# Transposing q and k of six batches on TensorE instead of by DMA, in an attention and GeGLU kernel

## The chip, the core and the metric

The kernel runs on one core of a Trainium2 chip. The core has TensorE (matmul; the trace shows its weight loads apart from its matmuls), VectorE, ScalarE, GpSimd and SyncE, which all run at once, each with an instruction queue of its own, and 16 DMA engines that serve the transfers that SyncE, ScalarE and GpSimd issue. The metric is the device time of one execution in microseconds (us).

## The reference

Two steps are computed. First comes attention with a sliding window and a linear distance bias, for 8 batches of 8 heads, 576 positions and a head size of 64; then a GeGLU block on the 4608 tokens.

```python
scores = (1/sqrt(64)) * q @ k.T
rel = pos[:, None] - pos[None, :]
scores = where((rel >= 0) & (rel < 128), scores - slope[h] * abs(rel), -1e9)
attn = softmax(scores)
x = (attn @ v)            # then laid out as [4608 tokens, 512]
out = (gelu(x @ w_gate) * (x @ w_val)) @ w_out    # 512 -> 1536 -> 512
```

All inputs and the output are float32; the kernel computes in bfloat16 with sums in float32.

## The kernel before

The tokens are cut into nine groups g of 512 (`NG`). For each group, a gate stage runs twelve steps f (`gate_val`, L615): eight matmuls of 512 columns each make 128 rows of the gate and the value, ScalarE applies gelu and VectorE multiplies, into `hid[g]`. After the gate stage comes a list of steps (`todo` for groups 0 and 1, `steps` for the others, L910 to L924). Numbers in the list are units of three output matmuls (`out_part`, L662); the named steps are the attention of later batches. In the list of group g from 2 on these are the weighted values of batch g + 1 (`pv`) and the scores of batch g + 2 (`s2`), so attention is ahead of the GeGLU block.

q and k of a batch are loaded by GpSimd in natural layout into `qs[b % 2]` and `ks[b % 2]`: five tiles of 128 positions, the fifth with 64, by 512 channels. The scores need them with channels on the partitions, as `qT[b % 2]` and `kT[b % 2]`: four column blocks c of 128 channels (two heads each) by 576 positions.

Batches 0 and 1 are transposed on TensorE, against the identity, at the start (`transpose`, L166, `first`, `rest`). For batches 2 to 7 `transposes_dma` (L173) issues six DMA transposes for a batch on SyncE's queue: five for q, one for each tile of 128 positions (L182), and one for k (L175), which lays the k blocks out by tile, so that `keys` (L195) picks them in another way. All five tiles are moved whole, so GpSimd first clears the unused 64 rows of the fifth (L904, L967). Batch 2 is transposed in the list of group 0, batch 3 at the start of group 1, and batch g + 2 at the start of group g, for g from 2 to 5.

The two buffers for each operand order the loads. GpSimd issues the loads of a later batch behind a small copy to `mark`, which waits for something: for the transposed q of batch 2 (L976) before the loads of batch 3, for the transposed k of batch 3 (L938) before those of batch 4, and for the product of step f = 9 (L960) before the later ones. In the same gate stages stand the sums of the softmax (`sums4`), their gathering and spreading by DMA on ScalarE's queue, and the loads at f = 9.

All matmul results go to eight banks of PSUM (`bank`, L68), one tile for each call; a bank is given out again when its last reader is done. The instructions run on each engine in the order written (a manual schedule); the framework adds the waits. SyncE's queue also carries the stores of the output (L659) and the small relays (L208) by which one half of a bank is handed from one pair of matmuls to another.

Of the kernel before, what the change touches and what calls it, by code (L numbers as in the profile page):

```python
# [8 lines left out]
BF16 = mybir.dt.bfloat16  # L9
# [23 lines left out]
def kernel(  # L33
# [10 lines left out]
    nc = tc.nc  # L44
    B, H, S, D = q.shape
# [22 lines left out]
    def bank():  # L68
        return psum.tile([128, 512], FP32, name="ps")


    def keep_busy(ps, n, w=64, rhs=None):
        for _ in range(n):
# [7 lines left out]
    ident = consts.tile([128, 128], BF16, name="ident")  # L81
# [11 lines left out]
    mark = consts.tile([1, 2], BF16, name="mark")  # L93
    last = consts.tile([128, DM], FP32, name="last")

    qs, ks = ([consts.tile([128, 5, DM], BF16, name=f"{nm}s{i}") for i in range(2)]
              for nm in "qk")
    qT, kT = ([consts.tile([128, 4, 640], BF16, name=f"{nm}T{i}") for i in range(2)]
              for nm in "qk")
    vb = [consts.tile([128, 5, DM], BF16, name=f"vb{i}") for i in range(2)]  # L100

    def rows(j):
        return 64 if j == 4 else 128
# [4 lines left out]
    def load(t, src, b, js=range(5), last=0):  # L108
        for j in js:
            n = rows(j)  # L110
            at = last if j == 4 else 0
            nc.gpsimd.dma_start(  # L112
                out=t[at:at + n, j, :].rearrange("p (h d) -> p h d", h=H),
                in_=src[b][:, 128 * j:128 * j + n, :].rearrange("h p d -> p h d"))

    def load_qk(b):
        load(qs[b % 2], q, b)
        load(ks[b % 2], k, b)

    def load_v(b, js=range(5)):  # L120
        load(vb[b % 2], v, b, js, 64)
# [44 lines left out]
    def transpose(b, what, c, copy):  # L166
        ps = bank().bitcast(BF16)
        for n, lo in ((0, 0), (1, 384)):
            transpose_runs(b, n, what, c, ps[:, lo:576])
        for n, lo in ((0, 0), (1, 384)):  # L170
            untangle(copy, b, n, what, c, c + 1, ps[:, lo:576])

    def transposes_dma(b):  # L173
        def of_k():
            nc.sync.dma_start_transpose(  # L175
                out=kT[b % 2].rearrange("p c (j t) -> p (c j) t", t=128),
                in_=ks[b % 2].rearrange("p j x -> p (j x)"))

        if b > 3:
            of_k()  # L180
        for j in range(5):
            nc.sync.dma_start_transpose(  # L182
                out=qT[b % 2][:, :, 128 * j:128 * j + 128], in_=qs[b % 2][:, j, :])
        if b <= 3:
            of_k()


    Ps = [consts.tile([128, H, 896], BF16, name=f"P{i}") for i in range(2)]
# [4 lines left out]


    def keys(b, c, m):  # L195
        if b < 2:
            return kT[b][:, c, 64 * m:64 * m + 64]
        at = 512 * (m // 2) + 128 * c + 64 * (m % 2)
        return kT[b % 2].rearrange("p c x -> p (c x)")[:, at:at + 64]

# [410 lines left out]
    hid = {}  # L613

    def gate_val(g, f, lo=0, hi=512, later=None):  # L615
        if g not in hid:
            hid[g] = h_pool.tile([128, NF, 512], BF16, name="hT")
        t0 = 512 * g % RING
        n = hi - lo

        if n > 256 or lo >= 384:
            pg, pv = bank()[:, 0:n], bank()[:, 0:n]
            order = [(w, ps, c, c == 0) for w, ps in ((wg, pg), (wv, pv)) for c in range(4)]
        else:
            ps = bank()
            pg, pv = ps[:, 0:n], ps[:, n:2 * n]
            order = [(w, ps, c, w is wg and c == 0)
                     for cs in ((0, 1), (2, 3)) for w, ps in ((wg, pg), (wv, pv)) for c in cs]
        cols = ((0, 256), (256, 512)) if (g, f) in HALVED else ((0, n),)
        for w, ps, c, begins in order:  # L630
            for a, e in cols:
                nc.tensor.matmul(  # L632
                    out=ps[:, a:e], lhsT=w[:, c, 128 * f:128 * (f + 1)], rhs=xT[:, c, t0 + lo + a:t0 + lo + e],
                    start=begins and a == 0, stop=(c == 3),
                    skip_group_check=n <= 256 and lo < 384 or len(cols) > 1)

        def act():
            gl = g_pool.tile([128, 512], BF16, name="gelu")
            nc.scalar.activation(out=gl[:, 0:n], in_=pg, func=AF.Gelu)  # L639
            nc.vector.tensor_tensor(out=hid[g][:, f, lo:hi], in0=pv, in1=gl[:, 0:n],  # L640
                                    op=ALU.mult)

        if later is None:
            act()
        else:
            later.append(act)
# [10 lines left out]
    def store():  # L657
        for args in stores:
            nc.sync.dma_start(**args)  # L659
        stores.clear()  # L660
# [63 lines left out]
    for h in (0, 2, 4, 6):  # L724
        for w, src in ((0, q), (1, k)):
            (nc.scalar if w and h == 0 else nc.sync).dma_start(  # L726
                out=raw[w][h // 4].rearrange("p (h x) -> p h x", h=4)[:, h % 4:h % 4 + 2, :],
                in_=src[0][h:h + 2, 0:384, :].rearrange("h (p r) d -> p h (r d)", r=3))
# [42 lines left out]
    def masks_of_last_blocks(lo, hi):  # L771
        nc.vector.tensor_copy(out=emask[:, lo:hi, 192:384], in_=emask[:, lo:hi, 0:192])
        nc.vector.tensor_copy(out=emask[:, lo:hi, 384:512], in_=emask[:, lo:hi, 0:128])
        for x, at in ((0, 128), (1, 0)):
            half = slice(64 * x, 64 * x + 64)
            nc.vector.tensor_copy(out=emask[half, lo:hi, 512:576], in_=emask[half, lo:hi, at:at + 64])


    act, dve = nc.scalar.copy, nc.vector.tensor_copy
# [64 lines left out]
    for do in inverse_a:  # L844
        do[1]()
    dve(out=pairs1.rearrange("p x (h d) -> p h x d", d=64),
        in_=vb[1].rearrange("p j x -> p (j x)")[:, 0:1536].rearrange(
            "p (h x d) -> p h x d", h=H, x=3))
# [6 lines left out]
    masks, waiting = [], []  # L855
# [39 lines left out]
    for n in range(4):  # L895
        nc.gpsimd.dma_start(
            out=wo[:, 3 * n:3 * n + 3, :],
            in_=moe_w_out[384 * n:384 * n + 384, :].rearrange("(c p) f -> p c f", p=128))
# [1 line left out]

    nc.gpsimd.memset(T[64:128, :, 0:64], 0.0)
    nc.gpsimd.memset(Ps[1][:, :, 0:64], 0.0)
    for t in (qs[0], ks[0]):
        nc.gpsimd.memset(t[64:128, 4, :], 0.0)  # L904
    load_qk(2)


    acts = (act, act, act, act)
    scales = []
    todo = {  # L910
        0: [("table",), ("s", 1, 0, (0, 1)), ("o", 0, 0, 0), ("o", 0, 1, 0), ("s", 1, 0, (2, 3)), ("o", 0, 0, 1), ("s", 1, 1, (0, 1)), ("o", 0, 1, 1), ("s", 1, 1, (2, 3), masks), ("pv+", 1, 0), 4, ("transposes", 2), ("pv+", 1, 1), 4],
        1: [("table",), ("s", 2, 0, (0, 1)), 3, ("s", 2, 0, (2, 3)), 2, ("s", 2, 1, (0, 1)), 2, ("s", 2, 1, (2, 3), masks), ("pv+", 2, 0, scales), 1, ("scale",), 2, ("pv+", 2, 1), 1, 2, ("s2", 3, 0), ("add", 3, 0), 3, ("s2", 3, 2), ("add", 3, 2, None, (0,))],
    }

    def steps(g):
# [11 lines left out]
    def exp_table():  # L927
        nc.scalar.preload_act_table_set("natural_log_exp_and_others")

    RUN = {"s": scores, "s2": scores2, "add": add, "sum4": sums4, "gather": gather, "spread": spread_dma, "pv": values, "pv+": values_and_sums,  # L930
           "masks": flush, "table": exp_table, "transposes": transposes_dma, "last": out_last, "scale": lambda: scales.pop()(), "o": out_half}

    for g in range(NG):
        if 1 <= g < B - 2:
            transposes_dma(3 if g == 1 else g + 2)
        if g == 1:

            nc.gpsimd.tensor_copy(out=mark, in_=kT[1][0:1, 0, 512:514])  # L938
            load_qk(4)
            load_v(3)  # L940
        for f in range(9 if g == 0 else 0, NF):
            gate_val(g, f)
            if g == 2 and f == 2:
                add(3, 2, act, (1,))
            if g == 0 and f == 10:
                masks_of_last_blocks(0, 8)
            if g == 0 and f == 9:
                for c in range(4):
                    for w in (0, 1):
                        transpose(1, w, c, (act, dve)[w])  # L950
            if 2 <= g < B - 1:
                if f == (4 if g == 2 else 3):
                    sums4(g + 1)
                if f == (6 if g == 2 else 5):
                    gather(g + 1)
                if f == (8 if g == 2 else 7):
                    spread_dma(g + 1)
                if f == 9 and g + 2 < B:

                    nc.gpsimd.tensor_copy(out=mark, in_=hid[g][0:1, f, 0:2])  # L960
                    if g + 3 < B:
                        load_qk(g + 3)
                    load_v(g + 2)
        if g == 0:
            nc.gpsimd.memset(Ps[0][:, :, 0:64], 0.0)
            for t in (qs[1], ks[1]):
                nc.gpsimd.memset(t[64:128, 4, :], 0.0)  # L967
        for item in steps(g):
            if isinstance(item, int):
                out_part(g, item)  # L970
            else:
                RUN[item[0]](*item[1:])
        store()
        if g == 0:

            nc.gpsimd.tensor_copy(out=mark, in_=qT[0][0:1, 0, 512:514])  # L976
            load_qk(3)
            load_v(2)

# [29 lines left out]
```

## Time and profile before

| what | value |
|---|---|
| median of 3 runs | 338.54 us (338.36 to 339.22) |
| the profiled execution | 337.69 us |
| span of its instructions | 335.9 us |
| TensorE busy | 327.7 us (98%), 3273 matmul records |
| VectorE, ScalarE, GpSimd busy | 192.9, 170.3, 108.3 us |
| granted TensorE clock | 1.00 |
| `qT<-qs` DMA transposes on SyncE's queue | 30, median 1258 ns to issue |
| `kT<-ks` DMA transposes on SyncE's queue | 6, median 3820 ns to issue |

The page of a profile counts how long each engine was busy and follows the chain of work that ended last. A line of a group names the source line, the engine, the operation, the tiles (out<-in), the shape and the number of instructions. For TensorE a form such as 128*64 gives the rows and columns of the array that the instruction uses. Matmuls are pipelined: one lasts 379 ns in the records where the next starts after 216 ns. Some records of matmuls are missing from the trace.

### The profile page before, as it was taken

The numbers are of one execution on the slowest core, as the hardware profiler recorded it, in microseconds if no ns is written. First come the engines' busy times: TensorE is split into PE (matmuls) and PEld (weight loads), VectorE is DVE, ScalarE is ACT, GpSimd is POOL, SyncE is SP. The second block draws the span as 40 slices with busy tenths as digits, with TensorE's granted clock in tenths as the row PEclk, the third lists the DMA queues.
The fourth block names the chain that finished last, engine by engine and source line by source line (L and its number), as shares of the span: only waits on it lengthen the run. The fifth ranks groups of instructions, "written<-read, shape, count | busy, mean of one in ns | idle before, by whom it ended". The sixth has DMA issues, their size and how long they took to land.

```text
span 335.9 us, 8087 instructions
## 1 busy us (share of the span) xinstructions
PE 327.7 (98%) x3273; PEld 169.5 (50%) x3316; DVE 192.9 (57%) x356; ACT 170.3 (51%) x318; POOL 108.3 (32%) x144
## 2 busy tenths in 40 slices
PE   8999999999999999999999999999999999999996
PEld 6667556444554454445544554445444544444444
DVE  7888776445779458845693469546964324303320
ACT  8974687438796339332943275335732233223322
POOL 6974784481193293009400860050000000000000
PEclk9999999999999999999999999999999999999999
DMA  8999999999999899969975999394105110020002
GB/s 216 170 197 191 205 164 189 117 181 137 183 161 153 181 184 198 164 161 134 184 163 104 153 187 179 81 166 83 64 3 140 64 65 0 1 96 31 0 31 96
DMA packets 149914, 43.49 MB, mean 129 GB/s; under 512 B 133588, under 2 KB 142836, under 8 KB 149876
## 3 DMA queue, kind: packets, MB, share of 16 engines
q0 software_dynamic: 107456, 18.10, 70.5%
q1 hardware_dynamic: 39104, 18.62, 25.4%
q10 hardware_dynamic: 3316, 6.25, 7.8%
q8 instruction: 26, 0.43, 0.5%
q14 instruction: 12, 0.10, 0.1%
HBM read 43.65 MB, written 9.53 MB: 158 GB/s over the span
## 4 chain that ended last, share of the span: by engine, by line
PE 94%; issue 2%; DMA 1%; DVE 1%; ACT 1%; SPq 0%; DVEq 0%
PE ps L632 56%; PE ps L669 25%; PE ps L501 5%; PE ps L298 2%; PE ps L689 2%; PE ps L216 1%; DMA qs<-in_q_dram 1%; PE ps L437 1%; PE ps L705 1%; PE ps L154 1%; ACT P L229 0%; SPq L726 0%; DVE xT L537 0%; DVE qT L162 0%; ACT rb L583 0%
## 5 line engine op out<-in xcount | busy, mean ns | idle before, releaser
L640 DVE TENSOR_TENSOR hT<-ps,gelu 128x512 bf16<-128x512 f32 (+3 forms) x117 | 73.6, 645 | 92.6 <-PE ps L632 86.0
L639 ACT ACTIVATE gelu<-ps 128x512 bf16<-128x512 f32 (+3 forms) x117 | 65.0, 564 | 101.7 <-PE ps L632 98.3
L632 PE MATMUL ps<-xT,wv 128*128 128x512 bf16 (+4 forms) x468 | 112.2, 361 | 0.4
L632 PE MATMUL ps<-xT,wg 128*128 128x512 bf16 (+4 forms) x456 | 111.2, 361 | 0.7
L669 PE MATMUL ps<-wo,hT 128*128 128x512 bf16 x375 | 87.6, 379 | 2.1 <-issue 1.4
L632 PEld LDWEIGHTS <-wv 128*128 128x128 bf16 x472 | 45.1, 98 | 48.6
L632 PEld LDWEIGHTS <-wg 128*128 128x128 bf16 x472 | 44.4, 98 | 47.6
L669 PEld LDWEIGHTS <-hT 128*128 128x128 bf16 x396 | 37.0, 98 | 43.4 <-issue 0.3
L229 ACT ACTIVATE P<-ps 128x512 bf16<-128x512 f32 (+1 forms) x108 | 51.3, 581 | 2.0 <-PE ps L216 1.5
L674 ACT COPY osb<-ps 128x512 f32<-128x512 f32 x27 | 15.9, 588 | 50.8 <-PE ps L669 50.8
L232 DVE TENSOR_TENSOR P<-P,emask 128x768 bf16<-128x768 bf16 x60 | 31.2, 555 | 18.2 <-ACT P L229 16.4
L112 POOL DMA_DIRECT2D vb<-in_v_dram x40 | 33.9, 886 | 6.5 <-DMA qs<-in_q_dram 2.3
L112 POOL DMA_DIRECT2D qs<-in_q_dram x30 | 25.2, 858 | 2.3 <-issue 1.8
L112 POOL DMA_DIRECT2D ks<-in_k_dram x30 | 25.4, 894 | 0.1
L960 POOL COPY mark<-hT 1x2 bf16<-1x2 bf16 x4 | 0.7, 174 | 75.7 <-DVE hT L640 75.7
L501 PE MATMUL ps<-P,vb 64*64 64x192 bf16 (+2 forms) x752 | 17.4, 220 | 0.4 <-issue 0.2
L565 DVE TENSOR_TENSOR xT<-ps,rb 128x512 bf16<-128x512 f32 (+3 forms) x34 | 14.6, 501 | 4.6 <-PE ps L501 4.6
L501 PEld LDWEIGHTS <-vb 64*64 64x64 bf16 x752 | 14.8, 107 | 3.6 <-issue 2.8
L385 DVE TENSOR_TENSOR T<-P 64x1024 bf16<-64x1024 bf16 x20 | 13.7, 686 | 0.6
L442 DVE RECIPROCAL r<-ps 128x128 f32<-128x128 f32 (+1 forms) x10 | 9.8, 1019 | 0.0
L298 PEld LDWEIGHTS <-kT 64*64 64x64 bf16 x440 | 7.5, 107 | 4.4 <-issue 4.4
L639 ACT ACT_TABLE_LOAD x7 | 9.0, 1283 | 1.3 <-PE ps L632 1.3
(93 smaller groups left out, 186.4 us busy)
## 6 DMA issues: line engine op xcount, KB each, us to landing
out_dram<-osb SPq DMA_DIRECT2D x35, 256.0 KB
rb<-rd ACTq DMA_DIRECT2D x10, 576.0 KB
vb<-in_v_dram POOLq DMA_DIRECT2D x32, 128.0 KB, 6.5
qs<-in_q_dram POOLq DMA_DIRECT2D x24, 128.0 KB, 5.5
ks<-in_k_dram POOLq DMA_DIRECT2D x24, 128.0 KB, 7.0
wo<-in_moe_w_out_dram POOLq DMA_DIRECT2D x4, 384.0 KB, 12.0
wg<-in_moe_w_gate_dram POOLq DMA_DIRECT2D x5, 256.0 KB, 8.5
wv<-in_moe_w_val_dram POOLq DMA_DIRECT2D x5, 256.0 KB, 9.3
```

Of the source, the lines that this page charges most:

```text
L112: nc.gpsimd.dma_start(out=t[at:at + n, j, :].rearrange("p (h d) -> p h d", h=H), in_=src[b][:, 128 * j:128 * j + n, :].rearrange("h p d -> ...
L229: nc.scalar.activation(out=dst, in_=src, func=AF.Exp, scale=0.125)
L232: nc.vector.tensor_tensor(out=dst, in0=dst, in1=m, op=ALU.mult)
L298: mm = nc.tensor.matmul(out=ps[64 * x:64 * x + 64, col:col + w], lhsT=keys(b, c, m)[half, :], rhs=qT[b % 2][half, c, q0:q0 + w], start=Tru ...
L385: nc.vector.tensor_tensor(out=to[half, :, x:x + 7:2], in0=P[half, :, 0:10:3], in1=P[half, :, 1:11:3], op=ALU.add)
L501: mm = nc.tensor.matmul(out=out, lhsT=lhsT, rhs=prob(b)[half, c, i, col:col + q1 - q0], start=all(t[2] != u for t in todo[:n]), stop=True, ...
L565: nc.vector.tensor_tensor(out=xT[:, c, at:at + e - a], in0=src, in1=recip[b][:, c, a:e], op=ALU.mult)
L632: nc.tensor.matmul(out=ps[:, a:e], lhsT=w[:, c, 128 * f:128 * (f + 1)], rhs=xT[:, c, t0 + lo + a:t0 + lo + e], start=begins and a == 0, st ...
L639: nc.scalar.activation(out=gl[:, 0:n], in_=pg, func=AF.Gelu)
L640: nc.vector.tensor_tensor(out=hid[g][:, f, lo:hi], in0=pv, in1=gl[:, 0:n], op=ALU.mult)
L669: nc.tensor.matmul(out=acc[g], lhsT=hid[g][:, f, 128 * t:128 * (t + 1)], rhs=wo[:, f, :], start=(f == 0), stop=(f == NF - 1))
L674: (nc.vector.tensor_copy if g < B - 2 and t in by_dve.get(g, (0,)) else nc.scalar.copy)(out=osb, in_=acc[g])
```

## The change

`transposes_dma` goes. In its place `transposes(b, c)` transposes column block c of q and of k on TensorE: for each of the two operands it takes a bank, issues five transposes against the identity (four of 128 positions, one of 64) and copies the 576 columns to `qT` or `kT`, the q block on ScalarE and the k block on VectorE (for two blocks of batch 3, both on VectorE). The calls stand in pairs inside gate stages: batch 2 after steps 5 and 7 of group 1, batch 3 after step 11 of group 1 and, one block at a time, in the list of group 1, and batch g + 2 after steps 6 and 8 of group g, for g from 2 to 5. `kT` has one layout for all batches, the clearing of the fifth tile's unused rows goes, and so does the mark before the loads of batch 3. The mark before the loads of batch 4 now waits for the product of step 11 of group 1.

```diff
-    def transposes_dma(b):
-        def of_k():
-            nc.sync.dma_start_transpose(
-                out=kT[b % 2].rearrange("p c (j t) -> p (c j) t", t=128),
-                in_=ks[b % 2].rearrange("p j x -> p (j x)"))
-
-        if b > 3:
-            of_k()
-        for j in range(5):
-            nc.sync.dma_start_transpose(
-                out=qT[b % 2][:, :, 128 * j:128 * j + 128], in_=qs[b % 2][:, j, :])
-        if b <= 3:
-            of_k()
+    def transposes(b, c, copies=None):
+        for w, (src, dst, copy) in enumerate(zip((qs, ks), (qT, kT), copies or (act, dve))):
+            ps = bank().bitcast(BF16)
+            for j in range(5):
+                n = rows(j)
+                nc.tensor.transpose(
+                    out=ps[:, 128 * j:128 * j + n], in_=src[b % 2][0:n, j, 128 * c:128 * c + 128],
+                    identity=ident[0:n, 0:n])
+            copy(out=dst[b % 2][:, c, 0:S], in_=ps[:, 0:S])
...
     def keys(b, c, m):
-        if b < 2:
-            return kT[b][:, c, 64 * m:64 * m + 64]
-        at = 512 * (m // 2) + 128 * c + 64 * (m % 2)
-        return kT[b % 2].rearrange("p c x -> p (c x)")[:, at:at + 64]
+        return kT[b % 2][:, c, 64 * m:64 * m + 64]
...
-    for t in (qs[0], ks[0]):
-        nc.gpsimd.memset(t[64:128, 4, :], 0.0)
     load_qk(2)
...
-        0: [..., ("pv+", 1, 0), 4, ("transposes", 2), ("pv+", 1, 1), 4],
-        1: [("table",), ("s", 2, 0, (0, 1)), 3, ("s", 2, 0, (2, 3)), 2, ("s", 2, 1, (0, 1)), 2, ...],
+        0: [..., ("pv+", 1, 0), 4, ("pv+", 1, 1), 4],
+        1: [("table",), ("s", 2, 0, (0, 1)), 3, ("transposes", 3, 2, (dve, dve)), ("s", 2, 0, (2, 3)), 2, ("transposes", 3, 3, (dve, dve)), ("s", 2, 1, (0, 1)), 2, ...],
...
     for g in range(NG):
-        if 1 <= g < B - 2:
-            transposes_dma(3 if g == 1 else g + 2)
-        if g == 1:
-
-            nc.gpsimd.tensor_copy(out=mark, in_=kT[1][0:1, 0, 512:514])
-            load_qk(4)
-            load_v(3)
         for f in range(9 if g == 0 else 0, NF):
             gate_val(g, f)
+            if g == 1 and f in (5, 7):
+                transposes(2, f - 5)
+                transposes(2, f - 4)
+            if g == 1 and f == 11:
+                transposes(3, 0)
+                transposes(3, 1)
+                nc.gpsimd.tensor_copy(out=mark, in_=hid[g][0:1, f, 0:2])
+                load_qk(4)
+                load_v(3)
+            if 2 <= g < B - 2 and f in (6, 8):
+                transposes(g + 2, f - 6)
+                transposes(g + 2, f - 5)
...
             nc.gpsimd.memset(Ps[0][:, :, 0:64], 0.0)
-            for t in (qs[1], ks[1]):
-                nc.gpsimd.memset(t[64:128, 4, :], 0.0)
...
         if g == 0:
-
-            nc.gpsimd.tensor_copy(out=mark, in_=qT[0][0:1, 0, 512:514])
             load_qk(3)
             load_v(2)
```

More of the change, by code (lines that the diff above doesn't have):

```diff
@@ L910 @@
     todo = {
-        0: [("table",), ("s", 1, 0, (0, 1)), ("o", 0, 0, 0), ("o", 0, 1, 0), ("s", 1, 0, (2, 3)), ("o", 0, 0, 1), ("s", 1, 1, (0, 1)), ("o", 0, 1, 1), ("s", 1, 1, (2, 3), masks), ("pv+", 1, 0), 4, ("transposes", 2), ("pv+", 1, 1), 4],
-        1: [("table",), ("s", 2, 0, (0, 1)), 3, ("s", 2, 0, (2, 3)), 2, ("s", 2, 1, (0, 1)), 2, ("s", 2, 1, (2, 3), masks), ("pv+", 2, 0, scales), 1, ("scale",), 2, ("pv+", 2, 1), 1, 2, ("s2", 3, 0), ("add", 3, 0), 3, ("s2", 3, 2), ("add", 3, 2, None, (0,))],
+        0: [("table",), ("s", 1, 0, (0, 1)), ("o", 0, 0, 0), ("o", 0, 1, 0), ("s", 1, 0, (2, 3)), ("o", 0, 0, 1), ("s", 1, 1, (0, 1)), ("o", 0, 1, 1), ("s", 1, 1, (2, 3), masks), ("pv+", 1, 0), 4, ("pv+", 1, 1), 4],
+        1: [("table",), ("s", 2, 0, (0, 1)), 3, ("transposes", 3, 2, (dve, dve)), ("s", 2, 0, (2, 3)), 2, ("transposes", 3, 3, (dve, dve)), ("s", 2, 1, (0, 1)), 2, ("s", 2, 1, (2, 3), masks), ("pv+", 2, 0, scales), 1, ("scale",), 2, ("pv+", 2, 1), 1, 2, ("s2", 3, 0), ("add", 3, 0), 3, ("s2", 3, 2), ("add", 3, 2, None, (0,))],
     }
@@ L930 @@
     RUN = {"s": scores, "s2": scores2, "add": add, "sum4": sums4, "gather": gather, "spread": spread_dma, "pv": values, "pv+": values_and_sums,
-           "masks": flush, "table": exp_table, "transposes": transposes_dma, "last": out_last, "scale": lambda: scales.pop()(), "o": out_half}
+           "masks": flush, "table": exp_table, "transposes": transposes, "last": out_last, "scale": lambda: scales.pop()(), "o": out_half}
     for g in range(NG):
-        if 1 <= g < B - 2:
-            transposes_dma(3 if g == 1 else g + 2)
-        if g == 1:
-            nc.gpsimd.tensor_copy(out=mark, in_=kT[1][0:1, 0, 512:514])
-            load_qk(4)
-            load_v(3)
         for f in range(9 if g == 0 else 0, NF):
             gate_val(g, f)
+            if g == 1 and f in (5, 7):
[10 more added lines that the diff above has]
+                transposes(g + 2, f - 5)
             if g == 2 and f == 2:
```

## The prediction

> **What bounds the kernel now.** I read the page first: who is busy, and who is on the chain that ends last.
>
> ```profile
> span 335.9 us, 8087 instructions
> PE 327.7 (98%) x3273; PEld 169.5 (50%) x3316; DVE 192.9 (57%) x356; ACT 170.3 (51%) x318; POOL 108.3 (32%) x144
> ...
> PEclk9999999999999999999999999999999999999999
> ...
> PE 94%; issue 2%; DMA 1%; DVE 1%; ACT 1%; SPq 0%; DVEq 0%
> ```
>
> TensorE works without a break and is 94% of the chain; no other engine passes 57%. A busy TensorE can still hide waits, so the waits of its two halves come next (matmuls, then weight loads).
>
> ```profile
> PE ps L669 <- issue: 1.4, 9, 0.2
> ...
> PEld L298 <- issue: 4.4, 11, 0.4
> ...
> PEld L501 <- SPq L209: 0.8, 3, 0.3
> ```
>
> No matmul of the stages waits for a DMA or for qT or kT of batches 2 to 7. The "issue" entries are no stalls: at each the start times show 320 ns in place of 95, which is one matmul record (216 ns) missing. After 20 us I find one stall of over 0.25 us, at 84.8 us. So what the change puts on TensorE inside a gate stage is paid in full, and what it takes from the DMA queues shortens nothing on TensorE. I then looked in the timeline of TensorE for what a transpose costs there, and what stands around it.
>
> ```profile
> 34.80 0.81 PE L632 MATMUL ps<-xT,wv 128*128 128x512 bf16 x3
> 35.55 0.25 PE L154 MATMUL ps<-ident,qs 128*64 128x128 bf16 x2
> ...
> 37.36 0.42 PE L154 MATMUL ps<-ident,ks 128*64 128x128 bf16 x10
> 37.72 0.39 PE L632 MATMUL ps<-xT,wg 128*128 128x512 bf16 x1
> ...
> 9.58 0.33 PE L784 MATMUL ps<-ident,qs 128*128 128x128 bf16 x3
> 9.74 0.33 PE L784 MATMUL ps<-ident,ks 128*128 128x128 bf16 x3
> 10.00 0.35 PE L501 MATMUL ps<-P,ones 64*64 64x384 bf16 x4
> ...
> 11.78 0.60 PE L797 MATMUL ps<-ident,wo 64*128 64x64 bf16 x24
> 12.31 0.35 PE L501 MATMUL ps<-P,ones 64*64 64x384 bf16 x1
> ```
>
> The first column is the start. Matmuls overlap, so their price is the distance between starts, not the duration. The pair 128*128, 128*64, 64*128 or 64*64 is the part of the array that the instruction uses, its tile shape. The reader is to see three prices.
> - A full transpose (weights 128x128, 128 columns of the identity): 9.58 to 9.74 is three, 53 ns each; single starts are 56 ns apart. I take 56.
> - A 64-row transpose (64*128): 24 of them take 11.78 to 12.31 with one change of shape, 18 ns each, but these run in pairs on the two halves of the array. One alone streams 64 columns where a full one streams 128, so I take 29 ns.
> - A change of shape. Three matmuls from 34.80 at 216 ns end their turn at 35.45, but L154 starts at 35.55; ten transposes from 37.36 take 255 ns, so L632 could start at 37.62, and starts at 37.72. In single start times such gaps are 93 to 98 ns, everywhere that the stream is dense: 128*128 to 64*64 and back, to 128*32 and back, to 128*64 and back, and 64*128 to 64*64. The weights of the next shape are loaded only once the array has let the old ones go, and the second matmul after a change is late by another 10 to 25 ns. I take 95 and 15.
>
> **The change part by part.** *Added on TensorE.* 6 batches x 4 column blocks x 2 operands = 48 groups, each of four full transposes and one of 64 rows (the last 64 of 576 rows): 192 and 48. The row of L797 says that 64 rows with 128 columns are a shape of their own, so each group changes shape before its fifth transpose and again after it: 96 changes. Three visits end just before 64*64 scores, where one change was there anyway (visits (3,0/1), (3,2), (3,3)): 93.
> - streams: 192 x 0.056 = 10.75 us, 48 x 0.029 = 1.4 us
> - changes: 93 x 0.095 = 8.8 us
> - late second matmul: 48 x 0.015 = 0.7 us
>
> Sum 21.7 us, all on the path, as TensorE has no idle time to put it in. Per batch that is 3.6 us, in two visits of 1.8.
>
> No row shows 128*128 next to 64*128 in a dense stream, so 95 ns is the one uncertain price. Its lower end is 0 (no drain between shapes that differ in rows alone): the sum is then 12.9. Its upper end is what the rows show for any pair, 98 plus 25 behind it: 22.6. A gain is excluded, since the change adds instructions to TensorE's queue and takes none from it. I take 95, since 64*128 to 64*64 measured 93 and the other shapes 95 to 97.
>
> The rate of a transpose stands against a rule. In the rows the transposes come 56 ns apart, and the stretch with 80 of them has a granted clock of 1.00 (windows view, the column after POOL):
>
> ```profile
> 35.40:37.80 2.40, 2.40 (x82) 2.19 (x82) 2.08 (x6) 1.77 (x7) 1.46 (x2) 1.00 1.29 200
> ```
>
> The Trainium skill (TensorE: Matmul & The Clock Gate, Part 4: PE-mode transpose) gives some 275 ns for a 128x128 bf16 transpose in a kernel and says that transposes do not count as busy for the clock. By that figure, an estimate, 240 transposes would be 66 us and the kernel some 404 us. The same skill (VectorE: DVE Perf Modes, The three transpose paths) ranks TensorE's transpose at 390 ns before the DMA's at 1309 ns; by that the change looks like a gain of speed, but the ranking leaves out that the DMA transposes here ran beside a full TensorE.
>
> *Added copies.* 22 on ScalarE and 26 on VectorE, 128x576 from PSUM. The copies of L162 take 549 ns (384 columns) and 346 ns (192) on VectorE, so 576 take some 750 ns; on ScalarE about 650 (476 to 512 and 362). In all 14 us of ScalarE and 19.5 us of VectorE: 184 and 212 us busy in a span of 358. They lie beside the matmuls: between two gate steps (8 x 0.216 = 1.73 us) ScalarE has one gelu of 0.60 and VectorE one product of 0.69, and a visit brings 1.8 us of TensorE with two copies on each. ScalarE then holds 1.9 of 3.5 us, VectorE 2.2. A visit takes 4 of the 8 banks, the next step needs those of the step before the last, which were read by then. If that cover were gone, a late copy would hold TensorE by at most its own 0.75 us, in 13 visits 9.8 us; the order of work gives no such case. The place to look at is the step list of g = 1, where the four copies of (3,2) and (3,3) queue on VectorE behind masks (0.56) and a 0.68 us copy of osb. VectorE is busy 12.25 of 18.1 us there, and needs 3.0 more in a stretch that grows by 1.8. ScalarE's exps set the pace there; they start 0.4 us later behind the two q copies of (3,0) and (3,1), then gain 1.8 us on TensorE. I set it at 0, bounds -0.3 (the stall at 84.8 goes) and +2.
>
> *Removed.* 36 DMA transposes on SP's queue (30 x 1.26 + 6 x 3.8 = 60.7 us of its time) and its waits for qs and ks. Behind them on SP stand stores and the relays of L209; TensorE's waits for relays sum to 0.8 us, all before 20 us, where SP has no transpose. Worth 0. On GpSimd four memsets (0.5 to 0.7 us) and two waits (9.0 and 12.7 us) go, so the loads of batch 3 start near 53 and not 63 us. Those of batch 4 now wait for VectorE's last product of gate stage 1, about 82 us and not 91; they take 8.4 us to issue and 7 to land, some 98 us, and their first transpose stands near 115. Batch 3 lands before 75 and is first read near 82. Later batches keep their place at f = 9, 30 us ahead. The weight load of a transpose therefore waits for no DMA: 0.
>
> **Sum.** The profiled execution took 337.69 us (span 335.9, 1.8 around it); 337.69 + 21.7 = 359.4. The median of the runs is 0.85 above the profiled one, so 360.2 us, 6.4% slower. A measurement of this kernel can tell about 0.3%, 1 us, from no change.
>
> **Rivals.**
> - *The drain is cheaper between 128*128 and 64*128.* For it: no dense row of this pair, and 96-row and 128-row transposes (96*64, 128*64) follow each other with no gap in L154. Against it: those two are one shape of the array, while the pairs of L797 show that 64 rows are not. At 0 ns the time is 351.4, at half price 355.8.
> - *The queue or the banks stop TensorE.* Each load of qs and ks lands in five parts; the weight load of each part waits for its own, and each group for a free bank. The two waits ahead of L154 stand in TensorE's queue as instructions of 51 ns. If 60 waits for landings and 48 for banks were each paid, 5.5 us; with the 2 us of g = 1, up to 367.7. Against it: in L154 they were passed 2 us earlier, as the queue runs ahead of the array. A quarter of it paid would be 362.
> - *Not slower.* TensorE would have to lose its extra streams in spare time: the weight port idles half the time, and L154's transposes run two at a time. It decides if at least 20.7 of the 21.7 us overlap. The price would be 0 to 1 us, so 337.7 to 339.5, with the 0.8 us of relays as the only gain. Against it: a 128*128 transpose uses the whole array, and the columns of the identity stream like any matmul's. Nor can faster gate matmuls pay for it: with the DMAs moving 158 GB/s (106 to 116 us) and nothing (306.4 to 316.4) the same 49 records take the same time.
>
> ```profile
> 105.87 10.74 PE ps L632 x49
> ...
> 306.35 10.74 PE ps L632 x49
> ```
>
> **How the numbers follow.** Full price 0.78, the cheaper drain 0.10, queue or banks 0.10, not slower 0.02. Predicted is the first, 360.2. The range reaches down to the half-priced drain and up to a good part of the waits, 355.5 to 364.0; below lie the free drain (0.06) and not slower (0.02), above it the rest of the waits (0.04). Faster by over 0.3%: 0.01; within: 0.01; slower: 0.98.
>
> **What would show it.** Two new groups on TensorE, weights of qs and ks with 128*128 and 64*128 forms; in the chain a piece of 1.8 us for each visit, 0.45 a group; gaps of 95 ns on both sides of each 64-row transpose; gate stages from g = 2 on 3.6 us longer (35.25 to 38.9 from one to the next); pieces of 10.74 us for 49 gate matmuls unchanged; clock 1.00. The first rival shows as visits near 1.1 us. The second shows as starts inside a group further apart than 56 ns, or waits of TensorE for copies. The prediction falls if the 64-row transposes do not change the shape, or if the clock drops in the visits.

## The result, and the profile after

| | before | after |
|---|---|---|
| median of 4 runs | 338.68 us (338.36 to 339.22) | 361.04 us (360.39 to 361.49) |
| profiled execution | 337.69 us | 361.49 us |
| span | 335.9 us | 359.7 us |

The ratio after to before is 1.0657, with a 95% interval of 1.0632 to 1.0682: slower by 22.4 us. Behind `keys` the line numbers of the kernel after are smaller by 7 (gate matmuls L625, output matmuls L662); the new transposes are L178, their copies L181.

The page of the kernel after answers the first question, whether TensorE still sets the time.

```profile
span 359.7 us, 8537 instructions
PE 349.9 (97%) x3508; PEld 184.7 (51%) x3556; DVE 203.4 (57%) x382; ACT 184.4 (51%) x340; POOL 105.6 (29%) x139
...
PEclk9999999999999999999999999999999999999999
...
q1 hardware_dynamic: 7232, 10.75, 8.5%
...
PE 94%; DMA 1%; issue 1%; DVE 1%; ACT 1%; SPq 0%; DVEq 0%
```

TensorE is busy 22.2 us longer and is again 94% of the chain. Queue q1 shows that the DMA transposes are gone: 7232 packets and 8.5%, where 39104 packets took 25.4%. That freed DMA time buys nothing on the chain.

Next the timeline of TensorE in one visit, that is, four groups of transposes between two gate steps (batch 5; first column the start, second the time from first start to last end).

```profile
156.31 0.52 PE L178 MATMUL ps<-ident,qs 128*128 128x128 bf16 x5
156.76 0.53 PE L178 MATMUL ps<-ident,ks 128*128 128x128 bf16 x5
157.22 0.53 PE L178 MATMUL ps<-ident,qs 128*128 128x128 bf16 x5
157.68 0.53 PE L178 MATMUL ps<-ident,ks 128*128 128x128 bf16 x5
158.14 0.61 PE L625 MATMUL ps<-xT,wg 128*128 128x512 bf16 x2
```

The visit lasts from 156.31 to 158.14, 1.83 us, and a group starts 0.46 us after the one before. Asked for a shorter stretch, the same view takes a group apart.

```profile
156.63 0.20 PE L178 MATMUL ps<-ident,qs 64*128 64x64 bf16 x1
156.76 0.53 PE L178 MATMUL ps<-ident,ks 128*128 128x128 bf16 x5
```

At the rate of the gate matmuls (512 columns in 216 ns) the 64-row transpose needs 27 ns for its 64 columns, but the next transpose starts 0.13 us after it: the rest is the change of shape. In single start times the 64-row transpose begins 150 to 153 ns after the full one before it, and what follows it begins 129 to 133 ns after it. Less 54 and 27 ns for the columns, the gap is 96 to 99 ns from 128*128 to 64*128 and 102 to 106 ns back, for all 96 changes. Inside a group the full transposes start 56 ns apart; behind a 64-row transpose the second of a group starts 67 ns after the first.

The view of L181 shows whether anybody waited for the copies (count, then shortest, median and longest in ns).

```profile
L181 DVE COPY kT<-ps x24: 449/457/459, 69.6 to 241.7; 128x576 bf16<-128x576 bf16 x24
L181 ACT COPY qT<-ps x22: 638/638/639, 69.1 to 241.2; 128x576 bf16<-128x576 bf16 x22
```

Its list of those who waited for it is empty. The windows over a visit show 1.00 as granted clock, with DMAs running (1.59 in the column after the clock) or not:

```profile
68.50:70.50 2.00, 2.00 (x22) 1.37 (x21) 1.16 (x3) 1.11 (x2) 0.00 (x0) 1.00 1.59 101
156.40:158.30 1.90, 1.90 (x22) 1.28 (x21) 1.20 (x3) 1.15 (x2) 0.00 (x0) 1.00 0.00 0
```

Laid side by side by the order of matmuls, from batch 1's transposes on, the two traces part only in the places of the change: ten visits between gate matmuls at 1.83 to 1.85 us, the visit before the scores of batch 2 at 1.74, the two of one block at 0.82 each, together 21.9 us. Two small stalls come to it: 0.35 us in the step list of group 1 (near 97 us) and 0.22 us in that of group 4 (at 211 us). The sum on TensorE is 22.4 us. The waits of TensorE's weight loads name what ended both stalls (us in total, times, longest):

```profile
PEld L494 <- SPq L202: 1.1, 4, 0.3
...
PEld L494 <- DVEq L202: 0.3, 1, 0.3
```

L202 is the relay that hands over one half of a bank. Before, SyncE's relays were waited for three times, 0.8 us, all before 20 us; the fourth is the stall at 211 us (0.23 us). The other, 0.30 us at 97.55 us, is a relay on VectorE's queue: the weighted values of batches 1 and 2 send theirs there and not on SyncE's. The profiled execution after was also 1.0 us later at the first transposes of batch 1 (36.59 and not 35.55 us). Over the profiled runs of this study that start lies between 35.5 and 36.6, so this is put down to spread and not to the change. The last 0.3 us of the 23.8 by which the spans differ lie behind the last copy.

### The profile page after: what moved, and what is told of

The parts are those of the page before. It is cut to its first block, busy times and chain, and to the rows that moved or that the text cites. A ratio compares the mean times of both kernels' runs of the same rounds, so it can differ in the third digit from the quotient of the medians.

```text
span 359.7 us, 8537 instructions
## 1 busy us (share of the span) xinstructions
PE 349.9 (97%) x3508; PEld 184.7 (51%) x3556; DVE 203.4 (57%) x382; ACT 184.4 (51%) x340; POOL 105.6 (29%) x139
## 3 DMA queue, kind: packets, MB, share of 16 engines
q1 hardware_dynamic: 7232, 10.75, 8.5%
## 4 chain that ended last, share of the span: by engine, by line
PE 94%; DMA 1%; issue 1%; DVE 1%; ACT 1%; SPq 0%; DVEq 0%
PE ps L625 52%; PE ps L662 24%; PE ps L178 6%; PE ps L494 5%; PE ps L291 2%; PE ps L682 2%; PE ps L209 1%; DMA qs<-in_q_dram 1%; PE ps L430 1%; PE ps L698 1%; PE ps L154 1%; ACT P L222 0%; SPq L719 0%; DVE xT L530 0%; DVE qT L162 0%
## 5 line engine op out<-in xcount | busy, mean ns | idle before, releaser
L625 PE MATMUL ps<-xT,wg 128*128 128x512 bf16 (+4 forms) x460 | 112.1, 361 | 0.8
L625 PE MATMUL ps<-xT,wv 128*128 128x512 bf16 (+4 forms) x460 | 111.2, 361 | 0.4
L662 PE MATMUL ps<-wo,hT 128*128 128x512 bf16 x374 | 87.6, 380 | 2.1 <-issue 1.4
L625 PEld LDWEIGHTS <-wv 128*128 128x128 bf16 x472 | 45.0, 98 | 48.7
L625 PEld LDWEIGHTS <-wg 128*128 128x128 bf16 x472 | 43.5, 98 | 45.8
L662 PEld LDWEIGHTS <-hT 128*128 128x128 bf16 x396 | 37.0, 98 | 43.3
L112 POOL DMA_DIRECT2D ks<-in_k_dram x30 | 25.4, 893 | 0.3 <-PE ps L625 0.3
L181 ACT COPY qT<-ps 128x576 bf16<-128x576 bf16 x22 | 14.0, 638 | 9.8 <-PE ps L178 9.8
L181 DVE COPY kT<-ps 128x576 bf16<-128x576 bf16 x24 | 11.0, 457 | 5.7 <-PE ps L178 5.1
L178 PE MATMUL ps<-ident,ks 128*128 128x128 bf16 (+1 forms) x120 | 12.7, 218 | 0.0
```

Of the source, the lines that this page charges most:

```text
L112: nc.gpsimd.dma_start(out=t[at:at + n, j, :].rearrange("p (h d) -> p h d", h=H), in_=src[b][:, 128 * j:128 * j + n, :].rearrange("h p d -> ...
L178: nc.tensor.transpose(out=ps[:, 128 * j:128 * j + n], in_=src[b % 2][0:n, j, 128 * c:128 * c + 128], identity=ident[0:n, 0:n])
L181: copy(out=dst[b % 2][:, c, 0:S], in_=ps[:, 0:S])
L625: nc.tensor.matmul(out=ps[:, a:e], lhsT=w[:, c, 128 * f:128 * (f + 1)], rhs=xT[:, c, t0 + lo + a:t0 + lo + e], start=begins and a == 0, st ...
L662: nc.tensor.matmul(out=acc[g], lhsT=hid[g][:, f, 128 * t:128 * (t + 1)], rhs=wo[:, f, :], start=(f == 0), stop=(f == NF - 1))
```

## The experiments

The theory: what the change costs is what TensorE streams (240 transposes) and, with nearly the same weight, the changes of tile shape around each 64-row transpose. The rivals: the visits wait for landings, banks or copies; and the removed DMA transposes had a price of their own, so that the change costs more than its net.

**All five tiles with 128 rows.**

```diff
             for j in range(5):
-                n = rows(j)
+                n = 128
...
+    for t in (qs[0], ks[0]):
+        nc.gpsimd.memset(t[64:128, 4, :], 0.0)
...
+            for t in (qs[1], ks[1]):
+                nc.gpsimd.memset(t[64:128, 4, :], 0.0)
```

> The fifth tile of q and k is transposed with all its 128 rows (cleared beforehand, as in the kernel before), so every transpose has the tile shape 128*128 and a group of five changes no shape. Theory (streams and shape changes on TensorE are the price): a group takes 5 x 56 ns = 0.28 us in place of the 0.463 us between group starts in the changed kernel, 240 x 0.056 = 13.4 us in all, so 338.7 + 13.4 = 352 us (351.5 to 353), and a visit of four groups about 1.13 us. Rival (the groups wait for landings, banks or copies): each group still waits, the gain is under 2 us and the time stays above 359 us.

Measured: 352.57 us (351.76 to 353.09), ratio to before 1.0412 (1.0392 to 1.0433). The timeline of a visit:

```profile
152.29 0.44 PE L178 MATMUL ps<-ident,qs 128*128 128x128 bf16 x5
152.57 0.44 PE L178 MATMUL ps<-ident,ks 128*128 128x128 bf16 x5
152.85 0.44 PE L178 MATMUL ps<-ident,qs 128*128 128x128 bf16 x5
153.13 0.44 PE L178 MATMUL ps<-ident,ks 128*128 128x128 bf16 x5
153.41 0.59 PE L625 MATMUL ps<-xT,wg 128*128 128x512 bf16 x2
```

A group now starts every 0.28 us, five times 56 ns, and the visit takes 1.12 us. It moves twice the columns in the fifth transpose and is faster by 0.18 us a group, 8.5 us in all. The waits that the rival needs are unchanged here (same landings, same banks, same copies), so they had no part in those 8.5 us.

**The 64-row transposes of a visit last.**

```diff
-    def transposes(b, c, copies=None):
-        for w, (src, dst, copy) in enumerate(zip((qs, ks), (qT, kT), copies or (act, dve))):
-            ps = bank().bitcast(BF16)
-            for j in range(5):
+    def transposes(b, cs, copies=None):
+        groups = [(src, dst, copy, c, bank().bitcast(BF16)) for c in cs
+                  for src, dst, copy in zip((qs, ks), (qT, kT), copies or (act, dve))]
+        for js in (range(4), (4,)):
+            for src, dst, copy, c, ps in groups:
+                for j in js:
...
+        for src, dst, copy, c, ps in groups:
             copy(out=dst[b % 2][:, c, 0:S], in_=ps[:, 0:S])
...
```

> The four groups of a visit first issue their sixteen full transposes, then the four 64-row ones, so a visit has two changes of shape in place of eight; the number and the shapes of the transposes stay. Theory: a visit of four groups takes 16 x 0.056 + 4 x 0.029 + 2 x 0.10 = 1.21 us in place of 1.83, one of two groups 0.71; 11 x 1.21 + 2 x 0.71 = 14.7 us, so 353.4 us (352.5 to 354.5). If it were the 64-row transposes themselves that are slow and not the changes around them, it would stay near 361.

Measured: 354.40 us (353.50 to 354.59), ratio 1.0460 (1.0438 to 1.0483). The end of a visit in its timeline:

```profile
153.70 0.39 PE L180 MATMUL ps<-ident,ks 128*128 128x128 bf16 x4
154.02 0.20 PE L180 MATMUL ps<-ident,qs 64*128 64x64 bf16 x1
154.06 0.19 PE L180 MATMUL ps<-ident,ks 64*128 64x64 bf16 x1
154.09 0.19 PE L180 MATMUL ps<-ident,qs 64*128 64x64 bf16 x1
154.12 0.19 PE L180 MATMUL ps<-ident,ks 64*128 64x64 bf16 x1
154.24 0.61 PE L627 MATMUL ps<-xT,wg 128*128 128x512 bf16 x2
```

The 64-row transposes follow each other at 0.03 to 0.04 us: they are cheap, and the gaps of 0.1 us stand only before the first and behind the last. Behind these four the change back takes 96 ns (next start 122 to 123 ns after the last), 10 ns less than behind a single one. The visit begins at 153.03 and takes 1.21 us, as expected. So it is the changes that cost, not the 64 rows. The whole came out 1.0 us above the expectation. Between batch 1's transposes and the sums of batch 3 the profile has 1.1 us that the visits do not explain (75.15 us, where the kernel without transposes, below, takes 69.27 and the visits add 4.74): 0.2 us before the scores of batch 2 and 0.9 us in the step list of group 1. In that list some scores of batch 2 come 0.4 us late (86.13 us), where the trace names ScalarE's exps, and a weight load waits 0.30 us for a relay on VectorE's queue (95.53 us), as in the changed kernel. I did not follow the rest.

**No transposes of batches 2 to 7 at all.** Their scores read stale qT and kT, so this kernel leaves out part of the computation.

```diff
     def transposes(b, c, copies=None):
-        for w, (src, dst, copy) in enumerate(zip((qs, ks), (qT, kT), copies or (act, dve))):
...
+        pass
```

> The transposes of batches 2 to 7 and their copies are left out, so the scores of these batches read what batches 0 and 1 left in qT and kT. Against the kernel before this shows what the DMA transposes, their waits and the cleared rows cost there. Theory: they cost TensorE nothing, 338.7 us (within 0.3%). Rival (the DMA transposes held the kernel before back by their traffic or on SyncE's queue, and the change wins that back): below 337.7 us, by as much as was won.

Measured: 339.24 us (338.33 to 340.44, 12 runs), ratio 1.0020 (1.0005 to 1.0035). The kernel without any transposes of these batches is not faster than the one with DMA transposes; if anything it is 0.5 us slower. So the DMA transposes, their packets and their waits on SyncE's and GpSimd's queues were hidden whole, and there was nothing for the change to win back. The two profiled spans differ by 1.0 us: 0.46 us of spread before batch 1's transposes, 0.22 us in the step list of group 4 and 0.3 us between the last copy and the end of the span. The 0.22 us are the stall of the changed kernel, a fourth wait for a relay on SyncE's queue:

```profile
PEld L486 <- SPq L194: 1.1, 4, 0.3
```

Why that relay comes later without DMA transposes is open, and so is whether these two pieces make up the 0.5 us of the medians.

**Each copy twice.**

```diff
-            copy(out=dst[b % 2][:, c, 0:S], in_=ps[:, 0:S])
+            for _ in range(2):
+                copy(out=dst[b % 2][:, c, 0:S], in_=ps[:, 0:S])
```

> Each copy of a group to qT or kT is issued twice in a row, which adds 22 x 0.64 = 14.0 us to ScalarE and 26 x 0.46 = 11.9 us to VectorE and nothing to TensorE. Theory: both engines have the room beside TensorE; 361.0 us, at most 361.8 by waits in the step list of group 1. Rival (copies and banks are what a visit waits for): up to 13 visits x 1 us, 365 to 374 us.

Measured: 361.68 us (360.87 to 362.24), ratio 1.0682 (1.0660 to 1.0704), 0.6 us above the changed kernel with ranges that overlap. The page shows that the work was there:

```profile
PE 353.6 (98%) x3556; PEld 185.1 (52%) x3556; DVE 214.4 (60%) x408; ACT 196.4 (55%) x362; POOL 105.6 (29%) x139
```

ScalarE is busy 12.0 us longer and VectorE 11.0 us; the time does not follow. The copies are not what a visit waits for, with room for as many again. Only in the step list of group 1 do they seem to count: from the scores of batch 2 to the sums of batch 3 this profile takes 29.26 us, and that of the changed kernel 28.86.

**Each full transpose twice.**

```diff
             for j in range(5):
                 n = rows(j)
-                nc.tensor.transpose(
+                for _ in range(2 if j < 4 else 1):
+                    nc.tensor.transpose(
...
```

> Each of the 192 full transposes is issued twice in a row to the same place; nothing else changes. Theory (each is streamed in turn, and nothing else ends its wait): 192 x 0.056 = 10.75 us more, 371.8 us (371 to 372.5), a group start every 0.69 us. Rival (a group waits for landings, banks or copies, so that streams hide in the waits): less than 5 us more, under 366 us.

Measured: 371.78 us (371.48 to 372.50), ratio 1.0975 (1.0954 to 1.0996): 10.74 us above the changed kernel, for 10.75 worked out. Pieces of its chain in order of time:

```profile
161.24 2.63 PE ps L179 x36
...
167.43 2.63 PE ps L179 x36
```

A visit of 36 transposes starts 0.2 us before its piece and takes 2.73 us, against 1.83: 16 more transposes, 0.9 us. Every transpose is paid at its streaming price.

**Each copy in two parts.**

```diff
-            copy(out=dst[b % 2][:, c, 0:S], in_=ps[:, 0:S])
+            for lo, hi in ((0, 384), (384, S)):
+                copy(out=dst[b % 2][:, c, lo:hi], in_=ps[:, lo:hi])
```

> Each copy of 576 columns is split into one of 384 and one of 192, the widths of the copies that batch 1 makes in both kernels, without the regrouping of columns that those make. The time should stay at 361 us. On VectorE the copies of batch 1 take 549 and 346 ns, from which the prediction worked out 750 ns for 576 columns, and the changed kernel shows 457. If the regrouping is what made those slow, the plain copies take about 330 and 200 ns; if the rate only rises with the width, they stay near 549 and 346.

One run: 361.62 us. The groups of the new copies (busy us, mean ns, then idle time before them):

```profile
L182 ACT COPY qT<-ps 128x384 bf16<-128x384 bf16 x22 | 10.5, 479 | 9.1 <-PE ps L178 9.1
L182 DVE COPY kT<-ps 128x384 bf16<-128x384 bf16 x24 | 8.6, 357 | 4.8 <-PE ps L178 4.2
L182 ACT COPY qT<-ps 128x192 bf16<-128x192 bf16 x22 | 7.1, 324 | 0.0
L182 DVE COPY kT<-ps 128x192 bf16<-128x192 bf16 x24 | 6.0, 248 | 0.0
```

On VectorE plain copies of 384 and 192 columns take 357 and 248 ns where those of batch 1, which regroup columns as they read, take 548 and 347 in the same kernel family. That is 0.57 ns a column against 1.05. ScalarE's plain copies (479 and 324 ns) are nearer to its regrouping ones (476 to 514 and 362 to 366). The shape of the read sets VectorE's price here, and the row that I had taken was of the other kind.

**Only k on TensorE, q by DMA.**

```diff
-        for w, (src, dst, copy) in enumerate(zip((qs, ks), (qT, kT), copies or (act, dve))):
+        for src, dst, copy in ((ks, kT, dve),):
...
+    def q_dma(b):
+        for j in range(5):
+            nc.sync.dma_start_transpose(
+                out=qT[b % 2][:, :, 128 * j:128 * j + 128], in_=qs[b % 2][:, j, :])
...
+        if 1 <= g < B - 2:
+            q_dma(g + 2)
         for f in range(9 if g == 0 else 0, NF):
```

> Only k is transposed on TensorE, in the places of the change; q goes by DMA as in the kernel before. 24 groups in place of 48. Theory (every group is paid for itself, and the DMA transposes cost nothing): 24 x 0.463 = 11.1 us over the kernel before, 349.8 us (349 to 350.6). If the price lay in the visits, in the landings of k (ks comes after qs) or in a part common to both operands, it would stay well above 352.

Measured: 349.83 us (349.38 to 350.29), ratio 1.0327 (1.0305 to 1.0350): 11.1 us over before, half of the price for half of the groups. Each group is paid for itself, and moving one back to the DMA gives its 0.46 us back.

Of the variants that transpose on TensorE, none comes near the kernel before: even without a change of shape, all of q and k cost 13.8 us there, and by DMA nothing. No experiment points to a version that beats the kernel before.

## Why the prediction was right

- *TensorE sets the time and nothing the change removes was on its path.* Right. Leaving the transposes out gave 339.24 against 338.74 us for the kernel before in the same runs, so the removed DMA transposes were worth nothing, as costed.
- *Streams, 12.15 us.* Right in price: 56 ns apart in the trace; doubling 192 of them cost 10.74 us for 10.75. As a price in a stream, the 275 ns of the Trainium skill (TensorE: Matmul & The Clock Gate, Part 4: PE-mode transpose) are not borne out: 56 ns, and the measurement decides. The granted clock was 1.00 in the visits, but these are at most 2.7 us long and lie between dense matmuls, so no run here tests the page's remark that transposes do not count as busy for the clock.
- *Changes of shape, 93 at 95 ns.* The uncertain price was taken from the neighbouring shapes and held: 96 to 99 ns one way, 102 to 106 ns back. So 9.4 us instead of 8.8. With the late second matmuls at 0.5 us, and 54 and 27 ns where the streams had 56 and 29, the visits come to 21.9 us for 21.7: these misses partly cancel, which is luck. Both experiments that took the changes away gave the time back. The upper end of the range for the visits, put at 22.6, adds up to 22.5 by its own terms.
- *Late second matmul, 0.7 us.* 11 ns each in a group, 0.5 us.
- *Copies at nothing.* Right, with one size wrong: VectorE's copies took 457 ns and not 750. I extrapolated from copies that regroup columns. It did not reach the time, as the copies are hidden either way; had they been on the path, that step would have been off by 7.6 us.
- *The step list of group 1 at 0, bounds -0.3 and +2.* It cost 0.35 us, by a relay on VectorE's queue, a wait that the prediction did not have: it counted SyncE's relays alone. How far the added copies hold that queue up is not settled: with each copy twice the list takes 0.4 us longer, but with each copy in two parts it takes 0.4 us less (28.48 us). In group 4, 0.22 us came that I had not looked for, by a relay on SyncE's queue. It appears without any transposes too, but not when q goes by DMA.
- *Loads.* The first loads of batch 3 are issued at 53.35 us as forecast, those of batch 4 at 84.1 for 82; no weight load of a transpose waited for a landing.
- *The sum.* 21.7 us predicted, 22.4 on TensorE in the trace; 360.2 predicted, 361.04 measured. Of the 0.7 us that were missing, 0.2 are in the visits and most of the rest are the two stalls.

The rivals: the cheaper drain falls by the gaps in the trace; queue or banks fall by the doubled copies and the doubled transposes, and what stalls there were (0.35 and 0.22 us) ended with relays and not with landings or copies; "not slower" falls by the time.

## What to carry to other kernels

In a kernel where one engine works 98% of the time, price a moved operation by the distance between starts on that engine, from rows of the same shape, and add what the switch to and from its shape costs; a transfer that nobody waited for gives nothing back when it goes. On TensorE a partial tile in a stream of full ones can cost more by its two changes of shape than a padded full one: here 0.18 us for each group of five. When a copy's price is taken from another copy, both must read in the same pattern.

## What the runs showed that I had not expected

- A change back from a single 64-row transpose, some 29 ns of work, costs slightly more than other changes: 102 to 106 ns, against some 96 behind four of them and 92 to 98 between other shapes in the same trace.
- VectorE copies bf16 from PSUM at 0.57 ns a column when it reads in order and at 1.05 when it regroups; on ScalarE the two differ by at most 13%.
- Taking 36 hidden DMA transposes away, with their waits and clearing, left the kernel 0.2% slower (1.0005 to 1.0035), not faster. In the profile a relay on SyncE's queue is then waited for, 0.23 us; why, and whether this is the cause, is open.
